# Halo rows, memsets, queues and a new plan in a fused long-convolution and linear-attention kernel

## The chip, the cores and the metric

The kernel runs on one core of a Trainium2 chip. The core has TensorE (matrix products, PE in the profile; its weight loads are PEld), VectorE (DVE), ScalarE (ACT), GpSimd (POOL), SyncE (SP, which here only issues DMAs), 16 DMA engines, a buffer SBUF of 128 partitions and an accumulator PSUM of 8 banks. The metric is the device time of one execution in microseconds; a lower number is better. The profile is of one execution.

## The reference

Two independent heads are computed and concatenated; S = 2048 rows, D = 576 channels, bf16.

```python
def _A_ref(q, k, v, shift_k, ssm_k, ssm_D):          # ks = 4
    k_pad = jnp.pad(k, ((0, 0), (ks - 1, 0), (0, 0)))
    k_shift = sum(k_pad[:, t:t + S, :] * shift_k[:, ks - 1 - t] for t in range(ks))
    kv = k_shift * v
    ...                                              # kv and ssm_k, zero padded to 2S
    y = irfft2(rfft2(kv_pad) * rfft2(kf_pad))[:S]    # a causal convolution over the rows
    y = y + kv * ssm_D
    return q * y

def _B_ref(x, wqkv, wo):                             # H = 32 heads of 18
    q, k, v = split(x @ wqkv)
    phi = lambda t: jnp.where(t > 0, t + 1, jnp.exp(t)) + 1e-6
    pq, pk = phi(q), phi(k)
    kv = einsum("bhsd,bhse->bhde", pk, v);  z = einsum("bhsd->bhd", pk)
    o = einsum("bhqd,bhde->bhqe", pq, kv) / (einsum("bhqd,bhd->bhq", pq, z) + 1e-6)
    return o.reshape(B, S, D) @ wo

return jnp.concatenate([a, b], axis=-1)
```

## The kernel before

Head A is a Fourier transform made of matmuls. A row number is n = 16 a + b, with a on the partitions and b = 0 to 15 in the free dimension. The filter ssm_k is loaded in six pieces `hs`, transposed on TensorE into `hT` (lines 379 to 400; D is added to its first row by an operation named hD), and goes through a first stage `s1` (matmuls with the table `Gsb`, line 413, evicted into `Ch`), a 32x32 transpose on VectorE (`ct`, line 433) and a second stage `s2` (matmuls with a small table in `idw`, line 443, evicted into `sph`), for three blocks of 192 channels and nine pieces of 64. The signal goes the same way: `conv_piece` (line 349 and behind it) makes kv from k and v. For each block and each half of the b's, two tap products of 3072 elements per partition (line 360, `m<-kh,Wj`), a sum of 3072, a sum of 1536 and a product with v. `kh` holds the rows of k with three rows more in front, the halo: `kh[p, 3:11]` are rows 16 p to 16 p + 7 and `kh[p, 0:3]` rows 16 p - 3 to 16 p - 1, which partition 0 has as zeros (a memset). The spectra are multiplied by two products of 2048 (`p1` with `sph`, `p2` with a copy `X` of it whose real and imaginary partitions are exchanged by two DMAs), the inverse runs through `i1` (line 479, into `V`) and `i2` (line 505, with the table `Esb`), and the result is multiplied by q (`yq`, or `i2q` straight from PSUM) and stored.

Head B transposes x on TensorE (line 303, into `xT`), projects k for 16 row blocks (line 545) and q for 4 x 5 blocks (line 566), makes phi with an exp on ScalarE and a scalar_tensor_tensor on VectorE (`pk`, line 553; `pqT`, line 572), forms x^T pk (`G`, line 594; `x_sb` and `pk` carry an extra column of ones and of eps), from it kv and M = kv wo, and a denominator. Its reciprocal `rden` (line 676) goes to DRAM (`r_scr`, two DMAs) and comes back spread over the partitions (`rb`, five DMAs, and one into `pqT`); five products on VectorE (`pqn`, line 228) normalize `pqT`, and 160 output matmuls (line 724) with their evictions `ob` and stores follow.

The order of the work is not left to a scheduler. All operations are recorded with their buffers (`Prog.op`), and `_issue` reads two long strings: PLAN has one word per operation, a letter for the engine (P, A, D, G, S) and its number, in the order in which the operations are issued; PLACES gives each buffer its address or PSUM bank. Each engine runs its own operations in that order and waits on semaphores for what it reads or overwrites. Operations listed for two engines ("DG", "AD") are put on one of them by the plan. Every DMA is one instruction in its engine's queue: a DMA that has to wait holds those behind it. `tt` (line 228) issues all two-input products, on VectorE or GpSimd; `copy` (lines 221 to 225) all evictions; `dma` (line 214) all DMAs. EARLY is the list of queues that the early loads may use, "SA" for SyncE or ScalarE; the plan put one piece of hs, Drow and one part of x on ScalarE.

Memsets are on GpSimd. That of the ones column of `x_sb` (line 265) and that of `pk`'s column (line 534) are recorded apart from the loads and products that write the other columns of the same buffers; in the plan the memset of x's column stands behind the first load of x, and the buffers' address ranges overlap.

Of the kernel before, what the change touches and what calls it, by code (L numbers as in the profile page):

```python
# [8 lines left out]
FP32 = mybir.dt.float32  # L9
# [169 lines left out]
def kernel(  # L179
# [47 lines left out]
    def tt(e, o, a, b, op):  # L227
        (nc.vector if e == "DVE" else nc.gpsimd).tensor_tensor(out=o, in0=a, in1=b, op=op)  # L228
# [5 lines left out]
    EARLY = "SA"  # L234
# [26 lines left out]
    P.op("G", lambda e: nc.gpsimd.memset(neg1.t[:], -1.0), wr=[neg1], name="neg1")  # L261
    for wx in (wk, wq):
        P.op("G", lambda e, wx=wx: nc.gpsimd.memset(wx.t[0:64, 4, :], 0.0), wr=[(wx, "t")], name="wz")
        P.op("G", lambda e, wx=wx: nc.gpsimd.memset(wx.t[96:128, 4, :], 1.0), rd=[(wx, "t")], wr=[(wx, "t")], name="w1")
    P.op("G", lambda e: nc.gpsimd.memset(x_sb.t[:, :, D:D + 1], 1.0), wr=[(x_sb, "o")], name="x1")
    P.op("G", lambda e: nc.gpsimd.memset(pqT.t[64:128, 4, :], 0.0), wr=[(pqT, (4, g)) for g in range(4)] + [(pqT, "r")], name="pqz")

    load("idw", idw, lambda e: dma(e, idw.t[:], C1_d), 128 * 320, 320, engs=EARLY)
# [6 lines left out]
    P.op("G", lambda e: nc.gpsimd.memset(ones.t[:], 1.0), wr=[ones], name="ones")  # L275
# [51 lines left out]
    def kv_load(bh):  # L327
# [5 lines left out]
        if bh == 0:  # L333
            P.op("G", lambda e: nc.gpsimd.memset(kh.t[0:1, 0:3, :], 0.0), wr=[(kh, "z")], name="khz")
            load("khh", kh, lambda e: dma(e, kh.t[1:128, 0:3, :].rearrange("p a d -> p (a d)"), ap(k, 13 * D, [[16 * D, 127], [1, 3 * D]])),
                 438912, 3456, wr=[(kh, "h")])
# [12 lines left out]
    def conv_piece(cc, bh):  # L349
# [4 lines left out]
        def tap(e, i):  # L354
# [5 lines left out]
            nc.vector.tensor_tensor(out=m.t[:, i:i + 2], in0=i0, in1=i1, op=ALU.mult)  # L360
# [131 lines left out]
    def inv2(gi):  # L492
# [5 lines left out]
        for bg in range(16 // nb):  # L498
# [10 lines left out]
            if gi in YA:  # L509
# [5 lines left out]
                def mul2(e, bg=bg, yb=yb):  # L515
                    qs = qb.t[:, nb * (bg - 1):nb * (bg + 1), c0:c0 + n]
                    tt(e, qs, yb.t[:], qs, ALU.mult)
# [16 lines left out]
    P.op("G", lambda e: nc.gpsimd.memset(pk.t[:, :, D:D + 1], EPS), wr=[(pk, "e")], name="pke")  # L534

    def kproj(r):
# [5 lines left out]
        def mm(e):  # L542
# [12 lines left out]
            in1=ps.t[:, :, 0:HALF], op0=ALU.min, op1=ALU.max), rd=[ps, eb], wr=[(pk, r)], name="kphi", n=576, st=st)  # L555
# [57 lines left out]
    P.op("G", lambda e: nc.gpsimd.memset(wv5.t[:, 4, :], 0.0), wr=[(wv5, "t")], name="wvz")  # L613
# [234 lines left out]
```

## Time and profile before

| | us |
|---|---|
| median of 3 runs (lowest, highest) | 210.91 (209.96, 211.08) |
| profiled execution | 210.5 |
| its span, first to last instruction | 208.5 |
| TensorE busy | 165.7 |
| VectorE busy | 149.8 |
| ScalarE busy | 133.0 |
| GpSimd busy | 57.7 |

In a row of the profile, "out<-in" are the kernel's tiles with buffer numbers left out, then come partitions and elements; in the timeline the first number is the start in microseconds from the span's start and the second the duration; brackets hold the idle time in front on that engine and what ended it. "SPq" is an issue on SyncE, "ACTq" on ScalarE. In the chain of waits a row is start, duration, and what the end of the kernel waited for in that time. In the rows by window, the columns are the window, its length, the busy time of each engine with its number of instructions, the granted TensorE clock, the share of the 16 DMA engines and the rate. A busy TensorE includes waiting inside its pipeline, so sums of single durations are larger than the time that they take back to back.

### The profile page before, as it was taken

How to read it: one execution, taken by the hardware profiler on the slowest of the kernel's cores; microseconds unless marked ns; L12 is line 12 of the kernel's file. 1: busy time of each engine (PE TensorE's matmuls, PEld its weight loads, DVE VectorE, ACT ScalarE, POOL GpSimd, SP SyncE). 2: the span in 40 equal slices, each digit the busy share in tenths (PEclk: the TensorE clock that was granted, in tenths of full speed). 3: DMA queues.
4: the chain of work that ended last, by engine and by line, in shares of the span. 5: the costliest groups of instructions: out<-in, count | busy, mean ns of one | idle time of the engine just before them, and what ended most of it. 6: DMA issues, size and time to landing. Idle time of an engine off the chain costs nothing.

```text
span 208.5 us, 4202 instructions
## 1 busy us (share of the span) xinstructions
PE 165.7 (79%) x1718; PEld 126.0 (60%) x1718; DVE 149.8 (72%) x167; ACT 133.0 (64%) x237; POOL 57.7 (28%) x36
## 2 busy tenths in 40 slices
PE   0626999401999999999999994769999991499992
PEld 0516876301386566766856883559978991278871
DVE  0040994008589999999999999799999927983630
ACT  0133798500599998996899984659999993021432
POOL 8211100000500911438066090267025006600000
PEclk9999999955589999999999999699999998569999
DMA  6999538932002006800012402964371385063594
GB/s 186 281 344 336 124 93 271 310 122 78 11 5 101 2 3 221 304 12 3 0 53 92 163 2 35 334 222 158 134 321 36 111 232 157 0 167 116 134 323 170
DMA packets 17688, 30.07 MB, mean 144 GB/s; under 512 B 7525, under 2 KB 14310, under 8 KB 16774
## 3 DMA queue, kind: packets, MB, share of 16 engines
q1 hardware_dynamic: 17028, 28.84, 43.4%
q10 hardware_dynamic: 642, 0.98, 1.6%
q8 instruction: 13, 0.21, 0.5%
q14 instruction: 5, 0.04, 0.1%
HBM read 20.12 MB, written 4.98 MB: 120 GB/s over the span
## 4 chain that ended last, share of the span: by engine, by line
PE 34%; DMA 27%; DVE 20%; issue 8%; ACT 6%; SPq 2%; DVEq 0%; POOL 0%; ACTq 0%
DMA kh<-in_A_k_dram 14%; PE ps_all L724 10%; DMA x_sb<-in_B_x_dram 7%; DVE m L360 5%; DMA rb<-r_scr 4%; PE ps_all L594 4%; PE ps_all L479 4%; PE ps_all L566 4%; PE ps_all L413 4%; DVE ct L433 3%; DVE pqT L572 3%; DVE m L228 3%; PE ps_all L443 2%; SPq L214 2%; DMA r_scr<-rden 2%
## 5 line engine op out<-in xcount | busy, mean ns | idle before, releaser
L566 PE MATMUL ps_all<-xT,wq 128*126 128x512 bf16 (+1 forms) x100 | 26.8, 407 | 12.6 <-DVE hT L223 12.6
L360 DVE TENSOR_TENSOR m<-kh,Wj 128x3072 bf16<-128x3072 bf16 x12 | 20.6, 1752 | 13.0 <-DMA kh<-in_A_k_dram 12.9
L228 POOL TENSOR_TENSOR m<-m 128x1536 bf16<-128x1536 bf16 x4 | 12.4, 3098 | 53.0 <-DVE m L228 53.0
L566 PEld LDWEIGHTS <-wq 128*126 128x126 bf16 (+1 forms) x100 | 12.9, 139 | 21.3 <-DMA wq<-in_B_wqkv_dram 10.4
L228 POOL TENSOR_TENSOR sph<-spu,sph 128x2048 bf16<-128x2048 bf16 x4 | 17.0, 4261 | 27.1 <-ACT spu L221 15.8
L724 PE MATMUL ps_all<-M,pqT 126*128 126x288 bf16 (+1 forms) x160 | 22.5, 300 | 0.1
L221 ACT ACTIVATE ob<-ps_all 128x288 bf16<-128x288 f32 x19 | 7.3, 410 | 24.0 <-PE ps_all L724 24.0
L594 PE MATMUL ps_all<-pk,x_sb 128*128 128x289 bf16 (+1 forms) x160 | 22.3, 294 | 0.1
L550 ACT ACTIVATE ek<-ps_all,neg 128x576 bf16<-128x576 f32 x16 | 11.9, 747 | 16.2 <-DVE pk L553 12.6
L545 PE MATMUL ps_all<-wk,xT 128*128 128x288 bf16 x160 | 21.7, 286 | 0.4 <-DVE pk L553 0.4
L479 PE MATMUL ps_all<-Esb,sph 128*128 128x128 bf16 x144 | 20.1, 227 | 0.0
L413 PEld LDWEIGHTS <-Gsb 128*128 128x128 bf16 x192 | 16.9, 101 | 5.3 <-issue 3.1
L479 PE MATMUL ps_all<-Esb,X 128*128 128x128 bf16 x144 | 20.0, 226 | 0.0
L221 ACT ACTIVATE V<-ps_all 128x512 bf16<-128x512 f32 x31 | 18.6, 705 | 1.6 <-PE ps_all L479 1.6
L221 ACT ACTIVATE Cu<-ps_all 128x768 bf16<-128x768 f32 x21 | 17.5, 871 | 3.2 <-PE ps_all L413 2.6
L221 ACT ACTIVATE sph<-ps_all 128x512 bf16<-128x512 f32 x35 | 19.2, 611 | 0.1
L479 PEld LDWEIGHTS <-sph 128*128 128x128 bf16 x144 | 18.8, 149 | 0.8 <-issue 0.8
L724 PEld LDWEIGHTS <-pqT 126*128 126x128 bf16 (+1 forms) x160 | 16.1, 102 | 5.2 <-DVE pqT L228 0.6
L594 PEld LDWEIGHTS <-x_sb 128*128 128x128 bf16 x160 | 15.7, 101 | 5.7 <-issue 1.6
L479 PEld LDWEIGHTS <-X 128*128 128x128 bf16 x144 | 18.5, 149 | 0.2 <-issue 0.2
L545 PEld LDWEIGHTS <-xT 128*128 128x128 bf16 x160 | 15.4, 98 | 5.0 <-issue 1.1
L505 PE MATMUL ps_all<-V,Esb 128*128 128x192 bf16 x96 | 11.1, 257 | 7.2 <-DVE M L712 7.2
(84 smaller groups left out, 330.0 us busy)
## 6 DMA issues: line engine op xcount, KB each, us to landing
X<-sph SPq DMA_DIRECT2D x18, 256.0 KB, 6.9
v<-in_A_v_dram SPq DMA_DIRECT2D x2, 1152.0 KB
q<-in_A_q_dram SPq DMA_DIRECT2D x1, 2304.0 KB, 9.2
out_dram<-q SPq DMA_DIRECT2D x12, 192.0 KB
out_dram<-ob SPq DMA_DIRECT2D x16, 144.0 KB, 2.5
rb<-r_scr SPq DMA_DIRECT2D x4, 504.0 KB
hs<-in_A_ssm_k_dram SPq DMA_DIRECT2D x5, 384.0 KB
x_sb<-in_B_x_dram SPq DMA_DIRECT2D x3, 576.0 KB
```

Of the source, the lines that this page charges most:

```text
L221: nc.scalar.activation(out=o, in_=i, func=ACTF.Copy)
L228: (nc.vector if e == "DVE" else nc.gpsimd).tensor_tensor(out=o, in0=a, in1=b, op=op)
L360: nc.vector.tensor_tensor(out=m.t[:, i:i + 2], in0=i0, in1=i1, op=ALU.mult)
L413: nc.tensor.matmul(ps.t[:, bank, lo - 384 * bank:hi - 384 * bank], lhsT=Gsb.t[:, b, ri, :], rhs=src[:, lo - CC * j:hi - CC * j], start=Tru ...
L433: P.op("D", lambda e: nc.vector.transpose(out=ct.t[:].rearrange("p w r t -> p (w r t)").bitcast(FP32), in_=C.t[:, nw * pp:nw * pp + nw].re ...
L479: nc.tensor.matmul(o[:, 128 * c8:128 * c8 + 128], lhsT=view(src.t[:], 4 * hh + c8, [[16, 128]]), rhs=Esb.t[:, 32 + wi, :], start=(wi == 0) ...
L505: nc.tensor.matmul(ps.t[:, 0, n * j:n * j + n], lhsT=Esb.t[:, 2 * b + ri, :], rhs=V[gi].t[:, 2 * b + ri, :], start=(ri == 0), stop=(ri == 1))
L545: nc.tensor.matmul(ps.t[:, hh, 0:HALF], lhsT=xT.t[:, t, 128 * (r % 4):128 * (r % 4) + 128], rhs=wk.t[:, t, HALF * hh:HALF * hh + HALF], st ...
L550: P.op("A", lambda e: nc.scalar.activation(out=eb.t[:], in_=ps.t[:, :, 0:HALF], func=ACTF.Exp, bias=neg1.t[:]), rd=[ps, neg1], wr=[eb], na ...
L566: nc.tensor.matmul(ps.t[0:hn, 0, :], lhsT=wq.t[:, t, h0:h0 + hn], rhs=xT.t[:, t, :], start=(t == 0), stop=(t == 4))
L594: nc.tensor.matmul(ps.t[:, 0, 0:n], lhsT=x_sb.t[:, r, FT[t]:FT[t] + 128], rhs=pk.t[:, r, HALF * hh:HALF * hh + n], start=(r == 0), stop=(r ...
L724: nc.tensor.matmul(ps.t[:, 0, 0:HALF], lhsT=pqT.t[0:kn, c, 128 * r:128 * r + 128], rhs=M.t[0:kn, c, HALF * hh:HALF * hh + HALF], start=(c ...
```

## The change

Seven things change together; none is left out of the diff but repeated memset lengths.

1. EARLY is "S": all loads are issued by SyncE.
2. The halo load of k, 127 partitions at once, becomes two, of partitions 1 to 112 and 113 to 127.
3. The loads of x now name the ones column as something they read, so each waits for its memset, which the plan puts ahead of all of them (third on GpSimd). Likewise the memset of pk's column is recorded at the start and `kphi` names it.
4. A new operation `warm`, an Exp of one column on ScalarE, stands at the head of its list, so that the activation table is loaded then.
5. Every two-input product on GpSimd waits, by a semaphore, for the last two-input product that VectorE has in front of it in the plan. VectorE does not wait for GpSimd's.
6. Memsets carry a length (`ms`), which only the planner reads.
7. PLAN and PLACES are new. In the new plan the filter and x come in another order in the head (one piece of hs, then x, then wk, Gsb), kh and v later; the sums of taps on GpSimd are 3 instead of 4, the products with v 3 instead of 4, products with the spectrum 3 instead of 4, q products 4 instead of 3; the reciprocal stands some 50 entries earlier; the load of q is issued behind the loads of `rb`, just before the first output matmul; and the last three pieces of the inverse (`inv6` to `inv8`) stand among the output matmuls.

```diff
     def tt(e, o, a, b, op):
-        (nc.vector if e == "DVE" else nc.gpsimd).tensor_tensor(out=o, in0=a, in1=b, op=op)
+        return (nc.vector if e == "DVE" else nc.gpsimd).tensor_tensor(out=o, in0=a, in1=b, op=op)
...
-    EARLY = "SA"
+    EARLY = "S"
...
-    P.op("G", lambda e: nc.gpsimd.memset(x_sb.t[:, :, D:D + 1], 1.0), wr=[(x_sb, "o")], name="x1")
...
+    P.op("G", lambda e: nc.gpsimd.memset(x_sb.t[:, :, D:D + 1], 1.0), wr=[(x_sb, "o")], name="x1", ms=16)
+    P.op("G", lambda e: nc.gpsimd.memset(pk.t[:, :, D:D + 1], EPS), wr=[(pk, "e")], name="pke", ms=16)
...
+    warm = SB("warm", [128, 1], FP32)
+    P.op("A", lambda e: nc.scalar.activation(out=warm.t[:], in_=neg1.t[:], func=ACTF.Exp), rd=[neg1], wr=[warm], name="warm", n=1)
...
-             589824, 4608, wr=[(x_sb, g)], engs=EARLY)
+             589824, 4608, wr=[(x_sb, g)], rd=[(x_sb, "o")], engs=EARLY)
...
-            load("khh", kh, lambda e: dma(e, kh.t[1:128, 0:3, :].rearrange("p a d -> p (a d)"), ap(k, 13 * D, [[16 * D, 127], [1, 3 * D]])),
-                 438912, 3456, wr=[(kh, "h")])
+            for p0, p1 in ((1, 113), (113, 128)):
+                load("khh", kh, lambda e, p0=p0, p1=p1: dma(e, kh.t[p0:p1, 0:3, :].rearrange("p a d -> p (a d)"),
+                                                            ap(k, ((p0 - 1) * 16 + 13) * D, [[16 * D, p1 - p0], [1, 3 * D]])),
+                     (p1 - p0) * 3456, 3456, wr=[(kh, "h%d" % p0)])
...
-            in1=ps.t[:, :, 0:HALF], op0=ALU.min, op1=ALU.max), rd=[ps, eb], wr=[(pk, r)], name="kphi", n=576, st=st)
+            in1=ps.t[:, :, 0:HALF], op0=ALU.min, op1=ALU.max), rd=[ps, eb, (pk, "e")], wr=[(pk, r)], name="kphi", n=576, st=st)
...
-        cnt = 0
+        cnt, last = 0, None
         for o in order:
...
-            o.fn(o.eng)
+            ins = o.fn(o.eng)
+            ins = getattr(ins, "ins", ins)
+            if o.info.get("two"):
+                if o.eng == "DVE":
+                    last = ins
+                elif last is not None:
+                    tc.add_manual_dep(ins, last.name, mybir.DependencyInfo(mybir.DependencyClass.Sync, mybir.DependencyReason.SCHED_ONLY),
+                                      reason="products of VectorE and GpSimd one after the other")
 
 
 PLAN = """
-G221 S7 G1 G6 A403 P404 S348 S18 A11 P351 G50 G0 G5 P349 A25 P23 P21 G13 S397 A405 D22 G2 S342 P19 D352 S10 G3 S46
...
+G0 A8 G6 S344 S9 P345 P347 D348 G5 G1 A346 S11 G2 S20 P23 P21 D24 P25 D22 S13 S350 D26 G52 S49 P353 P351 S48 G3 S27
...
 """
 PLACES = """
-22272 150368 183456 175264 141664 69312 43456 145760 223584 169504 183488 184640 151040 203104 4 2 53952 5 4 3
...
+20640 150368 229312 151040 141664 27104 16512 145760 186624 179712 185472 192384 210848 159232 16512 0 0 31712 3 2
...
```

More of the change, by code (lines that the diff above doesn't have):

```diff
@@ L273 @@
     load("Esb", Esb, lambda e: dma(e, Esb.t[:].rearrange("p a c -> p (a c)"), E_d), 1114112, 8704)
-    P.op("G", lambda e: nc.gpsimd.memset(ones.t[:], 1.0), wr=[ones], name="ones")
+    P.op("G", lambda e: nc.gpsimd.memset(ones.t[:], 1.0), wr=[ones], name="ones", ms=128)
     for hh in range(2):
@@ L516, in mul2 @@
                     qs = qb.t[:, nb * (bg - 1):nb * (bg + 1), c0:c0 + n]
[L517 removed]
+                    return tt(e, qs, yb.t[:], qs, ALU.mult)
                 if bg % 2:
```

85 lines of the change are left out of this document (42 added, 43 removed), and 28 rows, old and new, of the table PLACES.

## The prediction

> **What bounds the kernel now.** I read the slices of the page first, to see where TensorE stands still, then the windows around those places, then the timeline and the chain of waits inside them.
>
> ```profile
> span 208.5 us, 4202 instructions
> PE 165.7 (79%) x1718; PEld 126.0 (60%) x1718; DVE 149.8 (72%) x167; ACT 133.0 (64%) x237; POOL 57.7 (28%) x36
> PE   0626999401999999999999994769999991499992
> PEclk9999999955589999999999999699999998569999
> GB/s 186 281 344 336 124 93 271 310 122 78 11 5 101 2 3 221 304 12 3 0 53 92 163 2 35 334 222 158 134 321 36 111 232 157 0 167 116 134 323 170
> ```
>
> A slice is 5.2 us. TensorE has four gaps: the first 17 us, 39 to 52, around 130, and around 177. Between them it is full, and VectorE with 149.8 us of work is nearly as full. So the price of a gap is its own length, and no edit can shorten the full stretches much.
>
> ```profile
> core 0: us, PE busy (x) PEld busy (x) DVE busy (x) ACT busy (x) POOL busy (x), PEclk, DMA share, GB/s
> 9.00:17.50 8.50, 2.32 (x20) 2.05 (x20) 2.22 (x4) 2.58 (x3) 1.97 (x5) 1.00 1.05 336
> 39.00:51.50 12.50, 0.04 (x1) 0.22 (x2) 3.99 (x4) 0.56 (x2) 0.00 (x0) 0.63 0.45 157
> 52.10:57.30 5.20, 5.20 (x21) 1.91 (x19) 2.99 (x3) 2.64 (x4) 3.09 (x1) 0.50 0.03 11
> 51.50:154.60 103.10, 97.23 (x1003) 68.87 (x1003) 97.54 (x100) 86.38 (x148) 38.70 (x13) 0.95 0.31 108
> 182.00:205.00 23.00, 22.85 (x175) 17.51 (x175) 11.76 (x26) 6.97 (x19) 0.00 (x0) 0.92 0.63 188
> ```
>
> The row 39.00:51.50 is the largest gap: 0.04 us of matmul in 12.5 us. The row behind it (52.10:57.30) is a second cost of it: the clock is 0.50, so 5.2 busy us do about 2.6 us of work.
>
> **The change, part by part.** Durations are of the profiled execution (210.5 us for its span of 208.5; the runs' median is 210.91), so the sum is made on the span and 2.0 us are added.
>
> *Ones column ahead of the loads.*
>
> ```profile
> 8.99 0.17 POOL L265 MEMSET x_sb<- 128x16 bf16 x1 [3.68 <-DMA x_sb<-in_B_x_dram]
> 9.19 0.40 ACTq L214 DMA_DIRECT2D x_sb<-in_B_x_dram  x1
> 17.55 1.03 PE L303 MATMUL ps_all<-idw,x_sb 128*128 128x128 bf16 x8 [6.02 <-DMA x_sb<-in_B_x_dram]
> ```
>
> The memset waited for the first x load, the second load was issued only behind the memset, and TensorE waited 6.02 us for it. Now the memset stands third on GpSimd, with nothing in front but 0.2 us of memsets, and every x load waits for it alone. What is late next is the order of the queue: up to the end of Gsb stand 3.7 MB, which at the 300 GB/s or so of the first slices and the 336 of the row 9.00:17.50 are there by some 15 us, about when TensorE comes to it. I take -6.0; bounds 0 (the loads only exchange places) and -7.2 (with the memset's own share of the wait).
>
> *Halo rows in 112 and 15.*
>
> ```profile
> kh<-in_A_k_dram SPq DMA_DIRECT2D x1, 428.6 KB
> 18.77 10.23 SPq L214 DMA_DIRECT2D kh<-in_A_k_dram  x2
> 19.09 28.30 DMA kh<-in_A_k_dram
> 47.51 3.43 DVE L360 TENSOR_TENSOR m<-kh,Wj 128x3072 bf16<-128x3072 bf16 x2 [12.95 <-DMA kh<-in_A_k_dram]
> 51.46 2.29 PE L566 MATMUL ps_all<-xT,wq 128*126 128x512 bf16 x5 [12.58 <-DVE hT L223]
> ```
>
> 28.30 us for 428.6 KB are 15 GB/s, a twentieth of the 310 GB/s of the slice at 36 us: the 127 rows do not spread over the DMA engines, and the issue behind them stood 10.23 us. VectorE, in order, stood 12.95 us at the first product with kh; TensorE behind it 12.58. With 112 rows spread evenly the piece costs 387 KB / 310 GB/s = 1.2 us, and the 15 rows at worst 51.8 KB at 15 GB/s = 3.4 us. In the new queue kh has about 6.8 MB up to its end; the first four slices moved (186 + 281 + 344 + 336) GB/s x 5.2 us = 6.0 MB by 20.9 us, so at that rate it lands near 25, and the first product stands where TensorE has done 20 us of work, near 27. So the gap goes: -12.5, and -2.6 for the clock behind it. Bounds: 0, if the 112 rows move as the 127 did, and -15.1. [...]
>
> *All loads from SyncE, table loaded early.*
>
> ```profile
> 1.17 0.53 ACTq L214 DMA_DIRECT2D Drow<-in_A_ssm_D_dram  x1
> L221 ACT ACT_TABLE_LOAD x1 | 1.3, 1283 | 9.6 <-POOL ones L275 9.6
> 5.02 0.86 PE L390 MATMUL ps_all<-idw,hs 96*128 96x96 bf16 x8 [5.02 <-DMA hs<-in_A_ssm_k_dram]
> ```
>
> Three loads (one of hs, one of x, Drow) move from ScalarE's queue to SyncE's. The x load took 0.40 us there and Drow 0.53; with a like price for hs that is +1.4 us of issue on SyncE, in a head where the transfers and not the issues end last: 0, bound +1.4. The table load stood at 9.63 us, beside the x wait, and takes 1.3 us; at the start it stands beside the 5.02 us in which TensorE waits for its first load: 0, and if that cover were gone, 1.3.
>
> *GpSimd's products wait for VectorE's.*
>
> ```profile
> 117.05 1.22 DVE L228 TENSOR_TENSOR sph<-spu,sph 128x2048 bf16<-128x2048 bf16 x1
> 120.09 4.76 POOL L228 TENSOR_TENSOR sph<-spu,sph 128x2048 bf16<-128x2048 bf16 x1 [5.26 <-ACT spu L221]
> 120.84 5.10 DVE L228 TENSOR_TENSOR sph<-spu,sph 128x2048 bf16<-128x2048 bf16 x1
> 134.40 4.09 POOL L228 TENSOR_TENSOR sph<-spu,sph 128x2048 bf16<-128x2048 bf16 x1 [9.54 <-DVE spu L223]
> 136.19 3.37 DVE L228 TENSOR_TENSOR X<-spu,X 128x2048 bf16<-128x2048 bf16 x1
> 140.22 0.66 PE L413 MATMUL ps_all<-v,Gsb 128*128 128x192 bf16 x6 [1.69 <-DVE spu L223]
> ```
>
> The same product takes VectorE 1.22 us alone and 5.10 when GpSimd multiplies: it ends when GpSimd ends. That is 3.9 us at 121, and 2.15 at 136, behind which TensorE stood 1.69 for the next eviction. The wait itself holds only GpSimd, and VectorE can still run into a product that has begun; but the new plan leaves, behind each GpSimd product of the middle, as much VectorE work without two-input products as the product lasts (evictions, transposes, phi). What waits behind GpSimd is its own next product and the inverse transform that reads it, planned 8 us later. I take -6.0; bounds -8 and +4 (one such meeting more).
>
> ```profile
> L228 DVE TENSOR_TENSOR v<-m,v 128x1536 bf16<-128x1536 bf16 x2 | 1.9, 950 | 0.0
> L228 POOL TENSOR_TENSOR v<-m,v 128x1536 bf16<-128x1536 bf16 x4 | 12.4, 3104 | 9.1 <-ACT eq L569 8.9
> L228 DVE TENSOR_TENSOR q<-yb,q 128x768 bf16<-128x768 bf16 x5 | 2.7, 547 | 0.0
> ```
>
> GpSimd does one product less of each of three kinds (a sum of taps of 1536, the product with v, one with the spectrum) and VectorE one more: 0.95 + 0.95 + 1.22, less 0.55 for a q product that goes the other way, and some 0.5 less of evictions: +2, since VectorE is as full as TensorE.
>
> *The tail of the new plan.*
>
> ```profile
> 154.63 3.34 DVE L676 RECIPROCAL rden<-den 128x512 bf16<-128x512 f32 x1
> 158.73 4.22 DMA r_scr<-rden
> 148.11 0.36 SPq L214 DMA_DIRECT2D q<-in_A_q_dram  x1
> 163.00 4.27 SPq L214 DMA_DIRECT2D rb<-r_scr  x5
> pqT<-r_scr SPq DMA_DIRECT2D x1, 128.0 KB, 9.7
> 174.07 6.78 POOL L228 TENSOR_TENSOR q<-yb,q 128x768 bf16<-128x768 bf16 x3 [15.05 <-ACT yb L221]
> 174.62 4.74 DVE L228 TENSOR_TENSOR pqT<-pqT,rb 126x2048 bf16<-126x2048 bf16 x2 [0.96 <-DMA rb<-r_scr]
> 180.21 1.44 PE L505 MATMUL ps_all<-V,Esb 128*128 128x192 bf16 x8 [7.22 <-DVE M L712]
> q<-in_A_q_dram SPq DMA_DIRECT2D x1, 2304.0 KB, 9.2
> ```
>
> From the reciprocal to the last normalizer row are 3.3 us, then to 163.0 the write, then the loads to 177 (the last is issued behind the five, at 167.3, and lands 9.7 later): 22.4 us that no plan shortens. Behind it, two products met GpSimd's (4.74 for 2.4), and TensorE stood 7.22 us. In the new plan 19 us of TensorE's and 21 of VectorE's work up to the last normalizer product lie between the reciprocal and the first output matmul, GpSimd's q products come after, so of the 7.2 some 1.5 stay (22.4 + 0.2 less 21): -5.7. Bounds -7.2 and 0. But the q load, issued at 148 before, now stands behind these loads on SyncE, so it starts about when the first output matmul does and lands 9.2 us later; 8.7 us of matmul stand before its first reader: +1, bounds 0 and +9.
>
> *What the plan itself costs.* An in-order plan loses where a hand-over is later than planned: 103.1 us of the middle for 97.5 of VectorE work, 5.6 lost, of which 6 above are partly counted. Every hand-over is new now; I add +3, bounds 0 and +10. (Cut in stretches of 25 plan entries, with the busy time per instruction of these rows, the larger of TensorE's and VectorE's work up to the reciprocal sums to 103 us where each alone sums to 90; before, 109 where they were 95 and 97. That is the upper end.)
>
> Sum: 208.5 - 6.0 - 12.5 - 2.6 - 6.0 + 2 - 5.7 + 1 + 3 = 181.7, and with 2.0 around the span **184 us**.
>
> A count forward agrees. TensorE starts at 5 and is held by arrivals to about 7 us behind its own work, so 22 us of work are done near 29; the 90 us of VectorE's work up to the reciprocal take 92; 23 to the first output matmul; 28.5 us of TensorE's work, at the 1.05 of before's middle (103.1 for 97.2), make 30; then the 3.5 from 205 to 208.5 as now: 29 + 92 + 23 + 30 + 3.5 = 177.5, 179.5 with the 2.0. The two differ by the +3 and +1.
>
> **The rivals.**
>
> *The output stage becomes bound by DMA.* q (2.3 MB) and all stores (4.7 MB) fall into one stage, where the row 182.00:205.00 shows a share of 0.63 with stores alone. For: 2.3 MB more at 310 GB/s are 7.4 us. Against: 7.0 MB at the 323 GB/s of the last but one slice are 22 us, less than the 30 of the stage. If the first readers of q wait the full 9 us and VectorE stands with them: 184 + 7 = 191.
>
> *The middle does not close up.* Stretches alternate between TensorE and VectorE, the 103 above in place of 92 + 2: +9, 193. Against: before had the same pattern and took 103.1 where its stretches sum to 109, the 6 of GpSimd's meetings included.
>
> *The split does nothing for the hole.* The 112 rows move at 15 GB/s, 387 KB take 25 us, the hole stays: 184 + 12.5 + 2.6 = 199. [...] Against it stands the row: these rows ran at a twentieth of the rate, so here there is something to win by another count.
>
> *Slower.* GpSimd's wait makes its products serial with VectorE's: what ran beside VectorE now lies between VectorE's products, and their readers stand. 3 + 3 products of 3.1, 3 of 4.1 and 4 of 2.3 us are 40 us; if all were exposed, 224. It decides from 27 us of exposure, seven of ten. Against: all but one wait for a product that they read anyway or that ended long before.
>
> **How the numbers follow.** Forecast 184 (its own range 178 to 190): 0.56. DMA-bound output stage, 191: 0.14. Open middle, 193: 0.11. Hole stays, 199: 0.07. Serial GpSimd, 224: 0.05. Better than forecast, down to 174, when the last three costs are nil: 0.07. The range takes in the forecast and most of the two next cases: 176 to 195. A measurement here tells about 0.5% from no change; that bound lies between the cases, so faster 0.94, same 0.01, slower 0.05.
>
> **What would show it.** Right: kh lands within 10 us of its issue and no VectorE row waits over 3 us for it; no wait of 6 us for x; the slices of TensorE from the fourth on hold no digit under 5 before the last; no VectorE product of 2048 over 2.5 us beside a GpSimd one; the first output matmul near 145. Wrong: a VectorE or SyncE wait over 5 us that has no row above, most likely at the q products, or a low clock behind a new gap.

## The result

The changed kernel takes 174.74 us (median of 4 runs, 173.93 to 176.12) against 210.44 (209.06 to 211.08) for the kernel before in the same runs: a ratio of 0.832, 95% interval 0.825 to 0.839. It is faster, as forecast, and lies 9.3 us under the 184 of the forecast, 1.3 us under its range. The profiled execution is the slowest of the four, 176.12 us for a span of 174.3, so 1.4 us of what follows is above the median. Medians and spreads below are of all executions, while a ratio leaves out the slow ones (over 1.5% above the fastest of their kernel), so the two can differ by up to 0.8%.

The slices of the changed kernel's page (4.4 us each), to be read against those of before:

```profile
span 174.3 us, 4221 instructions
PE 160.0 (92%) x1718; PEld 123.1 (71%) x1718; DVE 143.8 (83%) x168; ACT 133.6 (77%) x238; POOL 46.9 (27%) x35
PE   0399999899999999999999999999995999999991
PEclk9999999999999999999999999999999699999999
GB/s 109 265 371 283 275 295 199 282 336 138 0 143 312 44 114 157 4 0 0 4 0 0 124 120 258 231 291 259 76 150 263 270 376 99 81 167 91 267 276 171
```

The hole at 39 to 52 and the gap near 130 are gone, and the other two have shrunk: what is left is the first 9 us, a dip to 5 before the output stage (the slice at 131 to 135) with one slice of low clock behind it, and the end. TensorE stands still for 14.3 us of the span where it stood 42.8 before. It is also 5.7 us less busy with the same 1718 matmuls; the low clock behind the gaps, which went with them, accounts for about that much (an estimate, slice by slice from the two pages' rows PE and PEclk). VectorE's busy time fell from 149.8 to 143.8.

The windows of the same kernel, columns as before:

```profile
9.00:17.50 8.50, 8.50 (x81) 7.25 (x80) 3.60 (x6) 3.59 (x5) 0.50 (x2) 1.00 1.06 328
39.00:51.50 12.50, 12.50 (x106) 9.77 (x105) 12.40 (x14) 12.16 (x19) 3.55 (x3) 1.00 0.26 78
110.00:132.00 22.00, 21.81 (x369) 18.45 (x368) 19.78 (x25) 21.82 (x43) 17.31 (x7) 1.00 0.64 217
132.00:158.00 26.00, 24.20 (x268) 20.53 (x267) 22.96 (x28) 16.07 (x36) 6.71 (x4) 0.93 0.65 196
```

39.00:51.50, which held 0.04 us of matmul, holds 12.50, and 9.00:17.50 holds 8.50 for 2.32. Of these four windows only 132.00:158.00 still loses time: 1.8 us of standing and a clock of 0.93.

The timeline of the changed kernel at the places that the prediction named:

```profile
8.47 2.32 PE L306 MATMUL ps_all<-idw,x_sb 128*128 128x128 bf16 x20 [2.42 <-DMA x_sb<-in_B_x_dram]
11.49 1.95 SPq L214 DMA_DIRECT2D kh<-in_A_k_dram  x2
29.77 1.76 DVE L365 TENSOR_TENSOR m<-kh,Wj 128x3072 bf16<-128x3072 bf16 x1 [0.86 <-DMA kh<-in_A_k_dram]
116.73 4.12 POOL L228 TENSOR_TENSOR sph<-spu,sph 128x2048 bf16<-128x2048 bf16 x1 [1.52 <-ACT V L221]
118.26 3.35 DVE L680 RECIPROCAL rden<-den 128x512 bf16<-128x512 f32 x1
121.63 1.23 SPq L214 DMA_DIRECT2D r_scr<-rden  x2
126.64 4.67 SPq L214 DMA_DIRECT2D rb<-r_scr  x5
133.21 1.22 DVE L228 TENSOR_TENSOR pqT<-pqT,rb 72x2048 bf16<-72x2048 bf16 x1 [2.77 <-DMA rb<-r_scr]
142.09 4.48 PE L728 MATMUL ps_all<-M,pqT 126*128 126x288 bf16 x35
```

The wait for x fell from 6.02 us to 2.42, VectorE's for kh from 12.95 to 0.86. The reciprocal starts at 118.26 where it started at 154.63. The copies of the normalizer (rb) still hold VectorE for 2.77 us, and the first output matmul comes at 142.09. GpSimd's products no longer meet VectorE's of 2048, each of which takes 1.22 us; one product of 768 still meets GpSimd's (1.65 us at 149.51, for 0.55).

### The profile page after: what moved, and what is told of

It reads as the page before. It is cut to its first block, busy times and chain, and to the rows that moved or that the text cites. A ratio compares the mean times of both kernels' runs of the same rounds, so it can differ in the third digit from the quotient of the medians.

```text
span 174.3 us, 4221 instructions
## 1 busy us (share of the span) xinstructions
PE 160.0 (92%) x1718; PEld 123.1 (71%) x1718; DVE 143.8 (83%) x168; ACT 133.6 (77%) x238; POOL 46.9 (27%) x35
## 4 chain that ended last, share of the span: by engine, by line
PE 72%; DMA 22%; issue 1%; DVE 1%; POOL 1%; ACT 0%; SPq 0%; DVEq 0%; POOLq 0%
PE ps_all L570 13%; PE ps_all L598 12%; PE ps_all L728 11%; DMA wq<-in_B_wqkv_dram 10%; PE ps_all L484 9%; PE ps_all L418 7%; PE ps_all L549 7%; DMA hs<-in_A_ssm_k_dram 6%; PE ps_all L448 5%; PE ps_all L510 5%; DMA x_sb<-in_B_x_dram 4%; DMA rb<-r_scr 3%; PE ps_all L713 1%; PE ps_all L633 1%; PE ps_all L669 1%
## 5 line engine op out<-in xcount | busy, mean ns | idle before, releaser
L570 PE MATMUL ps_all<-xT,wq 128*126 128x512 bf16 (+1 forms) x100 | 24.5, 382 | 0.1
L228 POOL TENSOR_TENSOR m<-m 128x1536 bf16<-128x1536 bf16 x3 | 9.3, 3113 | 50.9 <-ACT GT L609 45.2
L549 PE MATMUL ps_all<-wk,xT 128*128 128x288 bf16 x160 | 22.5, 294 | 0.0
L728 PE MATMUL ps_all<-M,pqT 126*128 126x288 bf16 (+1 forms) x160 | 21.5, 285 | 0.0
L598 PE MATMUL ps_all<-pk,x_sb 128*128 128x289 bf16 (+1 forms) x160 | 21.4, 286 | 0.0
L418 PEld LDWEIGHTS <-Gsb 128*128 128x128 bf16 x192 | 16.2, 98 | 3.8 <-issue 1.6
L221 ACT ACTIVATE V<-ps_all 128x512 bf16<-128x512 f32 x26 | 14.8, 628 | 4.5 <-PE ps_all L484 4.4
L221 ACT ACTIVATE spu<-ps_all 128x512 bf16<-128x512 f32 x32 | 17.2, 612 | 1.3 <-PE ps_all L448 1.1
L728 PEld LDWEIGHTS <-pqT 126*128 126x128 bf16 (+1 forms) x160 | 15.3, 97 | 3.6
L221 ACT ACTIVATE Cu<-ps_all 128x768 bf16<-128x768 f32 x22 | 17.5, 872 | 0.2
L221 ACT ACTIVATE Ch<-ps_all 128x768 bf16<-128x768 f32 x19 | 15.3, 858 | 0.0
```

Source lines behind the costliest of these rows:

```text
L221: nc.scalar.activation(out=o, in_=i, func=ACTF.Copy)
L228: return (nc.vector if e == "DVE" else nc.gpsimd).tensor_tensor(out=o, in0=a, in1=b, op=op)
L418: nc.tensor.matmul(ps.t[:, bank, lo - 384 * bank:hi - 384 * bank], lhsT=Gsb.t[:, b, ri, :], rhs=src[:, lo - CC * j:hi - CC * j], start=Tru ...
L549: nc.tensor.matmul(ps.t[:, hh, 0:HALF], lhsT=xT.t[:, t, 128 * (r % 4):128 * (r % 4) + 128], rhs=wk.t[:, t, HALF * hh:HALF * hh + HALF], st ...
L570: nc.tensor.matmul(ps.t[0:hn, 0, :], lhsT=wq.t[:, t, h0:h0 + hn], rhs=xT.t[:, t, :], start=(t == 0), stop=(t == 4))
L598: nc.tensor.matmul(ps.t[:, 0, 0:n], lhsT=x_sb.t[:, r, FT[t]:FT[t] + 128], rhs=pk.t[:, r, HALF * hh:HALF * hh + n], start=(r == 0), stop=(r ...
```

## The experiments

All medians are of 4 to 10 runs. A ratio is to the runs of the kernel before beside it, whose medians were 209.97 to 210.73. The runs are two ladders: the parts of the change one after another on the old plan, and single parts undone on the new one.

| kernel | us | lowest to highest | ratio, 95% interval |
|---|---|---|---|
| old plan + halo split | 195.49 | 193.55 to 196.63 | 0.928, 0.918 to 0.938 |
| old plan + ones column | 210.65 | 208.41 to 212.88 | 0.999, 0.994 to 1.004 |
| + split + ones | 193.15 | 192.09 to 193.93 | 0.920, 0.912 to 0.927 |
| + split + ones + wait | 184.45 | 183.92 to 186.16 | 0.877, 0.871 to 0.884 |
| + split + ones + wait + SyncE | 181.93 | 181.24 to 182.80 | 0.867, 0.862 to 0.872 |
| the change | 174.74 | 173.93 to 176.12 | 0.832, 0.825 to 0.839 |

**The halo split alone.** The old plan, with the 127 rows cut in 112 and 15:

```diff
-            load("khh", kh, ... ap(k, 13 * D, [[16 * D, 127], [1, 3 * D]])), 438912, 3456, wr=[(kh, "h")])
+            for p0, p1 in ((1, 113), (113, 128)):
+                load("khh", kh, ... [[16 * D, p1 - p0], [1, 3 * D]])), (p1 - p0) * 3456, 3456, wr=[(kh, "h%d" % p0)])
```

> The kernel before with the halo load in 112 and 15 rows as its only change, in the old plan. By the prediction's terms the gap of 12.5 us and the slow clock behind it (2.6) go: 210.4 - 15.1 = 195.3 us. Rival, the split is worth more, since every load queued behind the 127 rows was late too: 190 or less. Rival, the old plan has another wait behind this one (the q weights, v): 200 or more.

Measured 195.49, 14.5 us less than the 210.0 of the kernel before (15.1 by the ratio). The hole at 39 to 52 is closed:

```profile
39.00:51.50 12.50, 12.50 (x105) 8.54 (x104) 11.36 (x13) 11.70 (x18) 3.45 (x2) 1.00 0.11 42
```

So the 127 rows in one piece made that hole: nothing else was changed.

**The split undone in the new plan.** The changed kernel, with the 127 rows in one load again at the place of the 15.

> The changed kernel with the halo load as one DMA of 127 rows again, at the place in the queue of the 15 rows. By the prediction's terms 15.1 us come back: 189.8 us, with a kh wait of VectorE and the clock low behind it. Rival, the new plan issues kh 10 us earlier and has room for a slow one: 183 or less. Rival, the slow rows hold every load behind them in the new single queue: 195 or more.

Measured 193.26, 18.5 us more (ratio 0.919, 0.916 to 0.922). Windows of this kernel:

```profile
17.50:30.00 12.50, 4.30 (x40) 3.04 (x39) 5.24 (x7) 4.96 (x7) 0.35 (x1) 0.70 0.40 128
30.00:39.00 9.00, 0.00 (x0) 0.00 (x0) 0.00 (x0) 0.00 (x0) 0.00 (x0) 0.50 0.84 246
39.01 1.03 PE L306 MATMUL ps_all<-idw,x_sb 128*128 128x128 bf16 x8 [16.98 <-DMA x_sb<-in_B_x_dram]
```

The third line is from its timeline: here TensorE waits not for kh but for a load of x that stands on SyncE behind the slow piece: it is issued at 9.37, next after the 127 rows, and lands 29.6 us later. With every load on one queue, the slow load held those behind it: the issues of x and hs next to it stood 6.04 and 10.59 us. In the new plan the split is worth more than in the old.

**The ones column.** In the old plan the memset of x's ones column is put first on GpSimd, alone and behind the split:

```diff
 PLAN
-G221 S7 G1 G6 ... G50 G0 G5 P349 A25
+G5 G221 S7 G1 G6 ... G50 G0 P349 A25
```

> The kernel before with the memset of x's ones column ahead of all loads as its only change. By the prediction's term -6.0: 204.4 us, with the first x wait of TensorE (6.0 us) gone. Rival: the loads only exchange places in front of the 127 rows, and the arrival of kh still sets the time: 208 to 210.4.

> The kernel before with the split and the memset both, old plan. If the two terms add: 210.4 - 21.1 = 189.3 us. Rival, they overlap (the x wait only moves the start of what the DMA queue limits): the time of the split alone within 2 us.

Alone it is worth nothing measurable (210.65). Behind the split it is worth 2.3 us by the medians (195.49 to 193.15) and 1.8 by the ratios, whose intervals overlap, so the gain is not clear of noise; the two profiles agree with it, since TensorE's waits in front of x fall from 6.9 us to 5.3. The alone case, timeline on VectorE and window:

```profile
47.34 3.43 DVE L360 TENSOR_TENSOR m<-kh,Wj 128x3072 bf16<-128x3072 bf16 x2 [13.56 <-DMA kh<-in_A_k_dram]
0.00:17.50 17.50, 6.17 (x61) 5.54 (x62) 2.22 (x4) 2.69 (x3) 6.61 (x14) 1.00 0.93 276
```

TensorE does 1.5 us more in the first 17.5 us (4.67 before), and VectorE then waits 13.56 us for kh in place of 12.95: what the head gains, the next arrival takes back. Of the 7.2 us that TensorE waits in front of x (1.2 for the memset, 6.0 for the load) 5.5 stay, because x is then late for another reason, below.

**GpSimd's wait.** In the old plan with the two edits above, every product of GpSimd waits for the last one of VectorE before it; and in the changed kernel the waits are left out.

```diff
 old plan
-            o.fn(o.eng)
+            ins = o.fn(o.eng) ... tc.add_manual_dep(ins, last.name, ...)
 changed kernel
-                elif last is not None:
+                elif 0:
```

> As the run with split and memset, and GpSimd's products wait for VectorE's, old plan. If the wait itself ends the meetings of products, 6.0 us less than that run: 183.3 us, and no VectorE product of 2048 over 2.5 us. Rival, the wait holds only GpSimd and the room for it comes from the new plan: the same time within 1 us, meetings still there. Rival of the other side: GpSimd's results come late in a plan without room, 2 to 5 us slower than that run.

> The changed kernel without GpSimd's waits for VectorE's products (nothing else depends on these waits). If the wait keeps the products apart, meetings come back, 3.9 us or more: 178.6 us and a VectorE product of 2048 over 2.5 us. Rival, the places in the plan alone keep them apart: 174.7 us within 0.5.

8.7 us less in the old plan (193.15 to 184.45); 9.3 us more without it in the new one (184.05, 182.83 to 184.88; ratio 0.875, 0.869 to 0.880). So holding GpSimd costs less than the meetings did, and the places in the new plan alone do not keep the products apart. A meeting (a VectorE product that runs into one of GpSimd's) in the timeline of the changed kernel without waits, what it does to TensorE, and the window around it:

```profile
113.75 4.53 POOL L228 TENSOR_TENSOR sph<-spu,sph 128x2048 bf16<-128x2048 bf16 x1
114.28 5.08 DVE L228 TENSOR_TENSOR sph<-spu,sph 128x2048 bf16<-128x2048 bf16 x1
118.25 5.06 POOL L228 TENSOR_TENSOR X<-spu,X 128x2048 bf16<-128x2048 bf16 x1
120.38 0.80 PE L418 MATMUL ps_all<-v,Gsb 128*128 128x192 bf16 x4 [4.26 <-DVE den L674]
110.00:132.00 22.00, 17.74 (x271) 15.22 (x264) 19.50 (x20) 15.71 (x30) 15.51 (x6) 0.84 0.52 166
```

VectorE's product began at 114.28 and ended at 119.36, 1.08 us after GpSimd's ended at 118.28: it stood until GpSimd was through and then took its usual 1.22 to within 0.2 us. GpSimd's next one, begun at 118.25 in that time, took 5.06 for 4.12. TensorE stands 4.26 us behind the meeting. In that window TensorE is busy 4.1 us less than with the waits (17.74 for 21.81), and the clock falls to 0.84.

**All loads from SyncE.** Three kernels: the old plan with split, ones and wait, its three loads of ScalarE's queue moved to SyncE at the same places; the changed kernel with three loads moved to ScalarE at the same places; and with two of them, first of all on ScalarE.

```diff
 old plan (before_swo_sync)         changed plan (after_actq)      changed plan (after_actq_front)
-A404 ... A11 ... A25               -S13 S350 ... S27              -G0 A8 ... S13 S350
+S404 ... S11 ... S25               +A13 A350 ... A27              +A350 A13 G0 A8 ...
```

> The old plan with the halo split, the ones column ahead and GpSimd's waits (184.45 us), and its three loads of ScalarE's queue issued from SyncE at the same places of the plan. In the 184.45 us kernel the first tile of x is issued at 1.64 and another 576 KB of x from ScalarE at 1.74; TensorE reads the first at 11.15. In the changed kernel the first x is issued at 2.04, alone in its time, and read at 8.47. Theory 'one queue in the order of need': the first x lands some 2.5 us earlier, and the head's gap shrinks by as much: 180.5 to 183 us. Theory 'the plan': issuing engine does not matter, the new order of the loads and of TensorE's work does all of the 9.7 us left: 184 to 185.2 us.

> The changed kernel with three early loads (a piece of hs, a part of x, Drow) issued by ScalarE again, at their places in the plan. The prediction priced the move at 0: 174.7 us. Rival, two queues bring the head's loads earlier: up to 1.4 us faster. Rival, ScalarE's waits in order hold the loads: 1 us or more slower.

> The changed kernel with the second tile of hs (384 KB) and Drow issued from ScalarE's queue, but as ScalarE's first instructions, ahead of its table load and of its first evacuation; x stays on SyncE. When three loads stood on ScalarE at their plan places (180.75 us), hs was issued at 6.03 us, behind the evacuation that ends TensorE's first transposes, against 2.89 us on SyncE, and TensorE waited 4.0 us for it. Theory 'place in the queue': issued first, hs lands in time, 174 to 176 us. Theory 'two queues share the 16 engines': 384 KB ahead of the first x delay it by about 1.4 us (at the 265 GB/s of that slice): 176 to 177.5 us. Theory 'any load from ScalarE costs': near 180 us.

Old plan: 181.93, 2.5 us less (2.2 by the ratios). Changed plan with three loads on ScalarE: 180.75 (179.72 to 181.31; ratio 0.861, 0.857 to 0.864), 6.0 more. With two of them in front: 174.03 (173.12 to 177.07; ratio 0.828, 0.822 to 0.833), no difference. The first x transposes in the old plan without and with the edit:

```profile
11.15 2.29 PE L303 MATMUL ps_all<-idw,x_sb 128*128 128x128 bf16 x20 [3.21 <-DMA x_sb<-in_B_x_dram]
```

```profile
8.45 2.25 PE L303 MATMUL ps_all<-idw,x_sb 128*128 128x128 bf16 x20
```

In the first, 576 KB of x from ScalarE's queue, issued at 1.74, were under way beside the 576 KB issued at 1.64 that TensorE was waiting for, and both came late: their transposes start at 11.15 and 16.05, behind waits of 3.21 and 2.61 us. In the second the two are issued one after the other, at 2.10 and 3.02, and their transposes start at 8.45 and 11.25, the first 2.7 us earlier. TensorE's waits for x fall from 5.8 us to 0.6 with it, those for hs grow from 5.6 to 8.2, and the one in front of the output stage falls from 5.7 to 4.0; the profiles don't tell which of these the end of the kernel feels. And ScalarE and TensorE in the changed kernel with three loads on ScalarE:

```profile
5.48 0.81 ACT L221 ACTIVATE hT<-ps_all 128x768 bf16<-128x768 bf16 x1 [3.24 <-PE ps_all L395]
6.03 0.34 ACTq L214 DMA_DIRECT2D hs<-in_A_ssm_k_dram  x1
13.91 1.51 PE L395 MATMUL ps_all<-idw,hs 96*128 96x96 bf16 x16 [4.01 <-DMA hs<-in_A_ssm_k_dram]
```

The load of hs stood behind ScalarE's first evacuation, which waited for TensorE: issued at 6.03 us where SyncE issues it at 2.89, and TensorE stood 4.01 us for it. Issued ahead of the evacuation it costs nothing in the end: TensorE's first wait, for the identity, grows from 4.6 us to 6.7 beside it, and its wait of 2.4 for x goes. So it is not the queue that costs but what stands in front of the load on the engine that issues it, and which transfers run beside it. The second queue added no rate: over the first 17.5 us the old plan moves 265 GB/s with its three loads on ScalarE and 268 with all on SyncE.

**The table.** The changed kernel without its early exponential:

```diff
-    P.op("A", lambda e: nc.scalar.activation(out=warm.t[:], in_=neg1.t[:], func=ACTF.Exp), rd=[neg1], ...
+    P.op("A", lambda e: None, rd=[neg1], ...
```

> The changed kernel without the one-column exponential that loads ScalarE's table early. The table load stands in ScalarE's program as an instruction of its own ahead of the first evacuation, and it has 3.2 us of idle time there. Prediction's term (0, with the head's DMA waits as cover): 174.2 to 175.3 us. Rival (the cover is gone, the load stands behind the first transposes): 176.0 us, 1.3 us more.

174.33 (173.32 to 176.73; ratio 0.829, 0.823 to 0.835): no difference. ScalarE's timeline shows why:

```profile
0.74 1.28 ACT L221 ACT_TABLE_LOAD   x1 [0.74 <-PEq L843]
5.63 0.81 ACT L221 ACTIVATE hT<-ps_all 128x768 bf16<-128x768 bf16 x1 [3.60 <-PE ps_all L395]
```

Once no load stands in front of it on ScalarE, the table load comes at 0.74 us by itself, ahead of the evacuation that waits.

**The normalizer's round trip.** First made longer: in the changed kernel the reciprocal goes through a second buffer in DRAM before the copies are read.

```diff
-            dma(e, ap(r_d, i * S, [[512, 4], [2 * S, 32], [1, 512]]), rden.t[:])
+            dma(e, ap(r0_d, i * S, [[512, 4], [2 * S, 32], [1, 512]]), rden.t[:])
+            if i == 0: dma(e, r_d.rearrange("a b s -> (a b) s"), r0_d.rearrange("a b s -> (a b) s"))
```

> The changed kernel with the reciprocal written to a second DRAM buffer first and copied from there, one more round trip of about 4.9 us ahead of the output matmuls. If a gap in TensorE's work costs its length alone: 174.7 + 4 to 5 = 179 to 180 us. If the clock falls in it, as behind the other gaps, another 2 us or more of output matmul: 181.5 or more, and a granted clock under 0.9 in the 5 us behind the gap.

The copies are issued 5.9 us later (132.51 for 126.64), but 2.7 of that was there at the reciprocal (120.97 for 118.26), so the second trip took 3.2 us and not the 4.9 expected. The time is 181.39 (178.71 to 182.43), 6.7 us more by the medians and 5.0 by the ratio (0.856, 0.848 to 0.864). TensorE's wait before the output stage grows from 1.8 to 5.6 us:

```profile
PE ps_all L484 <- DVE V L223: 1.8, 1, 1.8
```

```profile
PE ps_all L485 <- DVE V L224: 5.6, 1, 5.6
```

The first is the changed kernel, the second the one with the longer trip (columns: total, times, longest). So the new plan has about 2 us less cover than the trip needs, and what is added is paid in full. The medians and the ratio fall on either side of what I had set apart; the clock decides. The windows of 5 us behind the wait, again of the changed kernel and of the longer trip:

```profile
135.10:140.10 5.00, 5.00 (x46) 3.33 (x46) 4.87 (x5) 2.66 (x5) 0.00 (x0) 0.66 1.07 267
```

```profile
141.60:146.60 5.00, 4.99 (x48) 3.32 (x48) 4.34 (x5) 2.24 (x5) 0.00 (x0) 0.68 1.08 245
```

The clock is as low behind 1.8 us as behind 5.6, so the longer wait costs its length and no further clock there. That is one execution of each, and a short wait does not always lower the clock: in the profile of the kernel without the early exponential the wait is 2.2 us and the clock from 132 to 158 is 1.00.

Then taken away, in both plans: the copies read x from DRAM, so that they needn't wait for the write. The first output is multiplied by x and not divided.

```diff
-            dma(e, rb.t[0:hn, :], ap(r_d, 14 * c * S, [[S, hn // 9], [0, 9], [1, S]]))
+            dma(e, rb.t[0:hn, :], ap(x, 14 * c * S, [[S, hn // 9], [0, 9], [1, S]]))
 before_swo_sync_free2 also, in the loop that sets the places:
+        if b.name == "rden":
+            p = 117952
```

> The old plan with the halo split, the ones column, GpSimd's waits and all loads on SyncE (181.93 us), in which the copies of the normalizer (rb) are read from x in DRAM and so don't wait for the 4.9 us that its write takes to land; the first output is then multiplied by x and not divided (left out: the division). In the 181.93 us kernel the first copy is issued 4.9 us behind the write (133.28 and 138.18), VectorE's products wait up to 3.4 us for them and TensorE 4.0 us behind. Theory 'the round trip is bare in the old plan': 3.5 to 5.5 us less, the clock behind the gap included: 176.5 to 178.5 us. Rival 'the plan's 7.2 us lie elsewhere': 180.5 to 182.3 us.

> The changed kernel with the same edit (the first output is multiplied by x and not divided). Its write is issued at 121.63, the copies at 126.64, the first product waits 2.8 us and TensorE 1.8 us. Theory 'the new plan covers most of the round trip': 1.5 to 2.5 us less, 172.2 to 173.5 us, so that the distance between the two plans shrinks from 7.2 us to 4 to 5. Rival 'the normalizer is as bare in the new plan': 3.5 to 5.5 us less, 169 to 171.3 us, and the distance stays.

> The same as before_swo_sync_free (181.35 us; the first output is multiplied by x and not divided), with rden in memory of its own. In before_swo_sync_free the copies were still issued at 137.40, 4.9 us behind the write at 132.49: in the old plan the first copy's tile lies on rden's memory, so that it waits for the write that reads rden, wherever it copies from. Now the copies should be issued at about 134, 3.5 us earlier. Theory 'the round trip is bare in the old plan': VectorE's second product waits 3.5 us less and TensorE's gap of 4.9 us shrinks by as much: 176.5 to 178.3 us. Rival 'something else holds the old plan's end': 180.5 to 182 us, with the gap where it is.

Old plan 181.35 (180.90 to 182.01; ratio 0.862, 0.855 to 0.869), new plan 172.65 (170.36 to 174.00; ratio 0.813, 0.804 to 0.823), old plan with rden moved 180.43 (178.93 to 181.50; ratio 0.863, 0.851 to 0.876). The first missed its aim. SyncE in the old plan with copies from x, and then with rden moved too:

```profile
132.49 1.23 SPq L214 DMA_DIRECT2D r_scr<-rden  x2
137.40 4.80 SPq L214 DMA_DIRECT2D rb<-in_B_x_dram  x5
```

```profile
135.01 1.23 SPq L216 DMA_DIRECT2D r_scr<-rden  x2
136.34 5.14 SPq L216 DMA_DIRECT2D rb<-in_B_x_dram  x5
147.44 1.23 DVE L230 TENSOR_TENSOR pqT<-pqT,rb 126x2048 bf16<-126x2048 bf16 x1 [2.82 <-DMA rb<-in_B_x_dram]
152.49 1.00 PE L509 MATMUL ps_all<-V,Esb 128*128 128x192 bf16 x8 [2.50 <-DVE M L716]
```

In the old plan the tile of the first copy lies on the memory of rden, so the copy waits for the write that reads rden, wherever it copies from: still 4.9 us. With rden elsewhere the copies follow the write at once. TensorE's wait falls from 4.0 us (4.9 in the first of these runs) to 2.5, and the median by 1.5 us, but the ratio's interval takes in that of the 181.93 us kernel, so this gain is not clear of noise. What is left of the wait is for the copies themselves, 2.3 MB right in front of their reader. In the new plan TensorE's wait of 1.8 goes, and 2.1 us by the medians, 3.9 by the ratios; these fall on either side of what I had set apart for theory and rival. So the distance between the two plans did not shrink, as I expected: it is 7.2 us with the trip and 7.8 without (7.4 and 10.5 by the ratios, with wide intervals). Better cover for the write of the normalizer alone is not what makes the new plan faster. Cover for the copies can be part of it: without the write the old plan still waits 2.5 us for them, the new one not at all.

**A better order of the first loads.** The changed kernel with the identity ahead of the first hs, and x ahead of srow:

```diff
-G0 A8 G6 S344 S9 ... S11 G2 S20
+G0 A8 G6 S9 S344 ... S20 S11 G2
```

> The changed kernel with two swaps of SyncE's first loads: the identity before the first hs, and the first x before srow. TensorE's first matmul waits 4.6 us for the identity (issued second, at 1.20 us) and its x transposes 2.4 us for x (issued fourth, at 2.04 us); each moves up by 0.4 us. Theory 'the head sets the end': 174.0 to 174.5 us, 0.3 to 0.8 us less. Rival 'hs or kh is then what is late': 174.7 us.

173.38 (171.79 to 176.44; ratio 0.823, 0.818 to 0.829). The median is 1.4 us lower and the intervals overlap: it can't be told from the change. The head did gain: x's transposes start at 6.67 for 8.47, and by 39 us TensorE has done 33.2 us of work for 30.4. The reciprocal came 2.9 us earlier and the copies as much, but TensorE's wait for them grew from 1.8 to 2.6: the tail takes a part back.

## Why the prediction was right and where it was wrong

The terms of the sum, with what the ladder measured for each (one order of adding them; another order would share them out otherwise):

| step | taken | measured |
|---|---|---|
| halo rows, with the clock behind the hole | -15.1 | -14.5 |
| ones column | -6.0 | -2.3 |
| GpSimd's wait | -6.0 | -8.7 |
| all loads on SyncE | 0 | -2.5 |
| moved products +2, tail -5.7, q +1, the plan's own cost +3, table 0 | +0.3 | -7.2 |
| sum | -26.8 | -35.2 |

The sum started at 210.5 and the kernels of the ladder at 210.0; with these the two columns give 183.7 and 174.8. The column measured goes by the medians; by the ratios the five steps are -15.1, -1.8, -8.8, -2.2 and -7.4.

*Halo rows: right*, in mechanism and size. The hole of 12.5 us is gone with 112 and 15. The 28.3 us of the row of before run from 19.09 to the landing of the last kh; the 127 rows were issued just ahead of that, at 18.77, so the 15 GB/s that I took are theirs only if they landed last. That they did not spread shows from 24 to 28 us, while the issue behind them stood (19.09 to 29.00):

```profile
24.00:28.00 4.00, 3.94 (x49) 2.90 (x47) 3.80 (x5) 2.77 (x5) 0.00 (x0) 1.00 0.08 31
```

A share of 0.08 is 1.3 of the 16 DMA engines, at 31 GB/s. That the 112 rows spread evenly and take 1.2 us was an estimate; no run shows that piece by itself. One mark failed: kh did not land within 10 us of its issue, but some 18 us after (11.49 to 29.77), with other loads in front of it on the queue (in the changed kernel the DMA engines' share is 1.05 from 9 to 30 us). VectorE came to it just then (0.86 us of wait). The other marks came: 2.42 us of wait for x, no slice of TensorE under 5 from the fourth to the last but one, no VectorE product of 2048 over 1.3 us, the first output matmul at 142. Of the signs of being wrong one does not tell: SyncE stood 33 us for a buffer before 97.4 us while TensorE was busy 70.98 us of the 71 from 39 to 110. The other, a low clock behind a new gap, came with the 0.66 behind the 1.8 us.

*Ones column: mechanism right, size wrong.* The memset was what held the second x, but the next load was late by nearly as much. The bound of 0, "the loads only exchange places", was nearer than the -6.0 that I took.

*GpSimd's wait: mechanism right, size too small*, 8.7 and 9.3 us, past the bound of -8. I counted the meetings that I quoted and the wait of TensorE behind one of them; the windows show that the clock behind such a wait falls too (0.84 in the row of 110.00:132.00 above), which I had counted for the hole but not here. A part is the tail's: in the old plan TensorE's wait in front of the output stage fell from 7.2 us to 5.7 in this step. One reading was inexact: VectorE's product does not end when GpSimd's does but 1.1 us behind it (125.94 and 124.85 in the rows of before). The rival of serial products (224) is refuted by both runs.

*All loads on SyncE: wrong.* I priced only issue time, 0 to +1.4, and wrote that the transfers end last in the head. That was the reason to look at them: two transfers of x from two queues were under way together at no higher rate (265 GB/s for 268), and the one that was needed came 2.7 us later. So here the second queue made the needed load later without any issue time being lost.

*What the plan itself costs: this is the step that failed*, with the q load and the moved products. I added +3 and +1 to a count that gave 177.5 without them (179.5 with the 2.0 around the span), counted +2 for the moved products, and took "every hand-over is new now" as a loss. The plan is 7.2 us faster than the old one with the same parts. The forward count was the better sum: 22 us of TensorE's work near 29 us (at 30.0 it had done 22.3), the first output matmul near 145 (142.1), 30 for the output stage (28.6), 3.5 behind (3.7). What it had too long is the middle: 92 us to the reciprocal where 88 were enough (from 30 to 118.3). The middle did not stay open: TensorE is busy 58.48 us of 58.50 from 51.5 to 110. The q load did not hold anything: the first q product, at 148.68, has no wait. VectorE did get 2.2 us more work (141.66 in the old plan with all the parts, 143.85 now), the +2 of the moved products, but TensorE is the bound with 92% and it cost nothing. The tail's wait fell from 7.22 us to 1.8, as forecast (1.5), but in the ladder 3.2 of that had come with the parts before the plan. So where the sum had +6 for these three costs, the runs show none of them, and beside the 2.2 us of the tail the plan gains 5 more, whose cause is open.

Where the 7.2 us lie, by windows (0 to 39, and 132 to 158) of the old plan with all parts, then the first of them of the change (its second is in the result):

```profile
0.00:39.00 39.00, 29.73 (x293) 23.20 (x294) 22.47 (x28) 22.91 (x33) 9.19 (x20) 0.91 0.93 288
132.00:158.00 26.00, 22.04 (x256) 19.19 (x255) 21.03 (x26) 17.14 (x38) 4.17 (x3) 0.87 0.40 123
```

```profile
0.00:39.00 39.00, 30.37 (x318) 22.97 (x319) 23.61 (x28) 24.80 (x36) 7.78 (x19) 1.00 0.98 268
```

Busy time by granted clock, as an estimate of work done, gives 27.1 and 30.4 us in the head, 19.2 and 22.5 (24.20 at 0.93) in front of the output stage: 3.3 us in each place. The first of the two does not hold for another execution of the old plan, the one with copies from x whose copies still waited for the write (181.35 us by its median):

```profile
0.00:39.00 39.00, 30.20 (x302) 23.68 (x302) 22.42 (x28) 23.25 (x34) 9.75 (x20) 1.00 0.92 288
132.00:158.00 26.00, 21.11 (x254) 18.31 (x252) 20.10 (x25) 16.68 (x39) 3.24 (x3) 0.93 0.44 123
```

Its head runs at a clock of 1.00 and is busy 30.20 us, within 0.2 of the change, so the 3.3 us of the head are the low clock of one execution, and nothing is shown for the order of the loads. What both executions of the old plan have is the wait in front of the output stage: 4.0 and 4.9 us, where the change has 1.8. So by these profiles 2 to 3 of the 7.2 us are a shorter wait for the normalizer's round trip. The other 4 to 5 stay open; the second execution shows 1.5 us of them as a TensorE that is busy longer with the same matmuls (161.5 for 160.0). What is shown is that the cover of the normalizer's write alone is not the cause.

Of the other rivals: no output stage bound by DMA (the page's last slices have 81 to 376 GB/s with TensorE full), no open middle, no hole. The last case, "better than forecast, down to 174, when the last three costs are nil", is what came, and had 0.07. Its reason covers only a part: the three costs at nothing give 178, and the rest comes from GpSimd's wait and the loads on SyncE, which gained 5.2 us more than I had taken, less 3.7 of the ones column, and from what the plan gained.

## What to carry to other kernels

Look at the share of the DMA engines while a load is under way: where it is as low as the 0.08 of the 127 rows here, another cut of its partitions is worth a run. Here 112 and 15 were worth 14.5 to 18.5 us; no run tells which other counts are as slow. Keep the loads of the head in the order in which they are read, on one queue whose engine waits for nothing else: here a second queue brought the load that was needed 2.7 us later, and an engine with work issued one at 6.03 us instead of 2.89. When a gap closes, look for the arrival that is late next before taking its length as the gain, and when two counts of the same sum differ by costs that no row shows, give the count without them its share of the chance.

## What was not expected of the hardware

- A product of VectorE that met one of GpSimd's stood for the whole rest of it and not for a share (5.08 us for 1.22, ended 1.08 behind it), and the next one there took longer (5.06 for 4.12); keeping them apart was worth 8.7 to 9.3 us of 184 to 193.
- Two loads of 576 KB on two queues at once brought the first of them 2.7 us later than one after the other.
- TensorE's clock was as low in the 5 us behind a wait of 1.8 us (0.66) as behind one of 5.6 (0.68), and at 1.00 behind one of 2.2 in another execution: what a short wait costs beyond its length differs between executions.
- The same 80 transposes of x take 6.8 us (243 ns each) in the change and 8.0 us (260 ns) in the old plan with all parts, where they stand in more and shorter rows in the timeline. From these two rows (the first is the changed kernel):

```profile
L306 PE MATMUL ps_all<-idw,x_sb 128*128 128x128 bf16 x80 | 6.8, 243 | 2.4 <-DMA x_sb<-in_B_x_dram 2.4
```

```profile
L303 PE MATMUL ps_all<-idw,x_sb 128*128 128x128 bf16 x80 | 8.0, 260 | 0.6 <-DMA x_sb<-in_B_x_dram 0.6
```

The clock is not the reason: the execution of the old plan with a clock of 1.00 in its head has 264 ns. No run tells whether the rows are.
